# Block means of the values in two column groups of TensorE, gathered by two copies a head pair

## Chip, cores, metric

One core of a Trainium2 chip runs the whole kernel. The metric is device time in microseconds (us) of one execution; lower is better. Besides the time, every execution has a mean granted TensorE clock: 1.0 is full speed. Values of 0.997 to 0.999 in the profiled runs are a half-clock stretch at the very end (in the kernel before, from 253.70 us of 254.62 on); they count as full clock.

## The reference, cut to what matters

```python
k_sum = k.reshape(B, H, nb, block, D).max(axis=3)      # (B, H, S, D) = (4, 8, 768, 64)
v_sum = v.reshape(B, H, nb, block, D).mean(axis=3)     # block = 32, nb = 24
scores = [masked scores with 15 neighbours each way, scores with k_sum + log(block)]
attn   = softmax(scores) @ concat([v, v_sum])
...    # then x = attn as (3072, 512), and a GEGLU block with a gated residual:
out    = x + sigmoid(x @ w_res) * ((gelu(x @ w_gate) * (x @ w_val)) @ w_out)
```

The change concerns `v_sum` of the first batch only: 24 means of 32 rows for each of 8 heads.

## The kernel before

A query tile has 128 "keys": 96 real ones (64 and 16 on each side, the rims) and 32 rows of which 24 are the block means. The first batch is prepared by hand in a prologue, before the steady run of gate and value matmuls (`g`, `vv`) starts. The block means of a head pair are 12 accumulating matmuls; `bmat` is a shifted selection matrix, so that they arrive in rows 96 to 119 of a PSUM tile:

```python
def vsum_pair(hp, pool, tag):                       # L278
    vs = pool.tile([128, 512], F32, tag=tag, name="vs")
    hs = slice(2 * hp, 2 * hp + 2)
    for t in range(NT):                             # NT = 12
        nc.tensor.matmul(vs[:, 0:2 * D], bmat[:, t:t + 4, :], vext[0][0:QT, t, hs, 0:D],
                         start=(t == 0), stop=(t == NT - 1))
    nc.scalar.copy(vblk[96:128, hs, 0:D], vs[96:128, 0:2 * D].rearrange("p (h d) -> p h d", d=D))

# order of issue in the prologue (cut; each engine runs its own part in this order)
s_step(0, 0, st) ... s_step(0, 1, st, tiles=s1)     # scores (PE), exp (ACT) -> P
keep_warm(2, *t_bank)                               # 2 filler matmuls, 512 columns each
vsum_pair(0, *t_bank)
s_step(0, 2, st)
keep_warm(2, *o_bank)
pair_rims(0)                                        # copies of V's rims, on VectorE
s_step(0, 3, st, MM2)
pair_rims(1)
vsum_pair(1, *o_bank)
pair_rims(2)
av_band(0); av_blk(0)                               # ao = P @ V: 96 keys, then the 32 block rows;
keep_warm(1, *t_bank)                               #   av_blk ends in rz, xn on VectorE
vsum_pair(2, *t_bank)
nc.scalar.activation(gate1[:], bias_t[0:1, :], AF.Gelu)   # loads the Gelu table early
av_band(1); av_blk(1)
...
pair_rims(3)
keep_warm(1)
av_band(2); av_blk(2)
vsum_pair(3, *o_bank)
xt_step(0, 0, st, **t_turn)                         # transposes of xn, copied by ScalarE
av_band(3)
xt_step(0, 1, st, **o_turn)
av_blk(3)
...                                                 # gate and value matmuls, xt_step 2 and 3
```

The softmax here doesn't subtract the row's maximum and nothing guards it: scores larger than these inputs give would overflow.

Of the kernel before, what the change touches and what calls it, by code (L numbers as in the profile page):

```python
# [9 lines left out]
BF16 = mybir.dt.bfloat16  # L10
# [5 lines left out]
def kernel(  # L16
# [11 lines left out]
    nc = tc.nc  # L28
    B, H, S, D = q.shape
# [9 lines left out]
    QT = 64  # L39
    NT = S // QT  # L40
    HT = NT // 2
# [11 lines left out]
    const = ctx.enter_context(tc.tile_pool(name="const", bufs=1))  # L53
# [7 lines left out]
    ps_o = ctx.enter_context(tc.tile_pool(name="ps_o", bufs=1, space=bass.MemoryType.PSUM))  # L61
# [6 lines left out]
    band = const.tile([128, 2, 128], BF16, name="band")  # L68
    vblk = const.tile([128, H, D + 1], BF16, name="vblk")
    bias_t = const.tile([128, 1], F32, name="bias_t")  # L70
    bmat = const.tile([QT, NT + 3, 32], BF16, name="bmat")
    bgrp = const.tile([QT, 3, 32], BF16, name="bgrp")
    warm = const.tile([128, 512], BF16, name="warm")
    gate1 = const.tile([1, 1], F32, name="gate1")
# [4 lines left out]
    vext = [const.tile([128, NT, H, VP], BF16, name=f"vext{i}") for i in range(2)]  # L79
# [59 lines left out]
    with tc.manual_schedule():  # L139
# [13 lines left out]
        def own_keys(m, n):  # L153
            for i in range(2):
                rows = m[i * BLK:(i + 1) * BLK]
                nc.vector.memset(bass.AP(tensor=m.tensor, offset=rows[:, 0, i:i + 1].offset,
                                         ap=[rows.ap[0], [34, n]]), 1.0 / BLK)
# [27 lines left out]
        nc.vector.memset(band[:], 0.0)  # L185
        vext_consts(0)
        nc.vector.memset(bmat[:], 0.0)
        own_keys(bmat[:, 3:, :], NT)
        nc.vector.tensor_copy(band[0:QT, 0, 33:128], ident[0:QT, 0:95])
        nc.vector.tensor_copy(band[QT:128, 0, 33:97], ident[QT:128, QT:128])  # L190
        for i, d in enumerate((1, 2, 4, 8, 15)):
# [86 lines left out]
        def vsum_pair(hp, pool, tag):  # L278
            vs = pool.tile([128, 512], F32, tag=tag, name="vs")
            hs = slice(2 * hp, 2 * hp + 2)  # L280
            for t in range(NT):
                nc.tensor.matmul(vs[:, 0:2 * D], bmat[:, t:t + 4, :], vext[0][0:QT, t, hs, 0:D],  # L282
                                 start=(t == 0), stop=(t == NT - 1))
            nc.scalar.copy(vblk[96:128, hs, 0:D], vs[96:128, 0:2 * D].rearrange("p (h d) -> p h d", d=D))

        def vsum_grp(b, pool, tag):
            vs = pool.tile([128, DM], F32, tag=tag, name="vs")
# [89 lines left out]
        def xt_step(u, ko, st, pool, tag, copy=nc.vector.tensor_copy):  # L377
            xp = pool.tile([128, TU], BF16, tag=tag, name="xp")
            for sub in range(NSUB):
                nc.tensor.transpose(xp[:, sub * 128:(sub + 1) * 128],  # L380
                                    st["xn"][:, ko, sub, :], ident[:])
            copy(st["xT"][:, ko, :], xp[:])
# [5 lines left out]
        def new_unit():  # L388
            return {"xn": upool.tile([128, KO, NSUB, 128], BF16, tag="xn", name="xn"),
                    "xT": upool.tile([128, KO, TU], BF16, tag="xT", name="xT")}  # L390


        def gv_mm(ps, w, st, fo, kos):
            for ko in kos:
                nc.tensor.matmul(ps[:, 0:TU], w[:, ko, fo * 128:(fo + 1) * 128], st["xT"][:, ko, :],  # L395
                                 start=(ko == 0), stop=(ko == KO - 1), skip_group_check=True)
# [75 lines left out]
        def keep_warm(n, pool=ps_s, tag="s"):  # L472
            wp = pool.tile([128, 2 if pool is ps_s else 1, 512], F32, tag=tag, name="wp")
            for _ in range(n):
                nc.tensor.matmul(wp[:, 0], warm[:, 0:128], warm[:], start=True, stop=True)

        mm, t_bank, o_bank = (ps_mm, "mm"), (ps_t, "t"), (ps_o, "ao")
        keep_warm(12)
        tk, tq, ao = {}, {}, {}
# [11 lines left out]
        st = new_unit()  # L491
        gvT = upool.tile([128, FO, TU], BF16, tag="gvT", name="gvT")

        def ao_tile(hp):
            ao[hp] = ps_mm.tile([128, NSUB, 2, D + 1], F32, tag="mm", name="ao")
# [14 lines left out]
        s_step(0, 1, st, tiles=s1)  # L510
        ao_tile(0)
        ao_tile(1)
        keep_warm(2, *t_bank)
        vsum_pair(0, *t_bank)
        s_step(0, 2, st)
        keep_warm(2, *o_bank)
        pair_rims(0)
# [4 lines that stand above are left out]
        av_band(0)  # L522
        av_blk(0)
        keep_warm(1, *t_bank)
        vsum_pair(2, *t_bank)
        nc.scalar.activation(gate1[:], bias_t[0:1, :], AF.Gelu)
        av_band(1)
# [8 lines left out]
        o_turn = dict(pool=ps_o, tag="ao", copy=nc.scalar.copy)  # L536
# [6 lines left out]
        def gv_part(fo, ko):  # L543
            gv_mm(gv[fo][0], w_gate, st, fo, (ko,))
            gv_mm(gv[fo][1], w_val, st, fo, (ko,))
# [2 lines left out]
        xt_step(0, 2, st, **t_turn)  # L548
        gv_part(0, 1)
        gv_mm(gv[1][0], w_gate, st, 1, (0, 1))  # L550
        xt_step(0, 3, st, **o_turn)
        gv_part(0, 2)
        gv_mm(gv[1][1], w_val, st, 1, (0, 1))
        gv_part(0, 3)
# [100 lines left out]
        for u in range(NU):  # L655
# [57 lines left out]
            else:  # L713
                nst = new_unit()
                (mid_out if u else first_out)(u, st, gvT, nst)
                st = nst
# [30 lines left out]
```

## Time and profile before

| | before |
|---|---|
| time | 256.33 us (256.27 to 256.56) |
| span of the profiled run, mean granted clock | 254.6 us, 0.998 |
| TensorE busy | 246.6 us (97%) |
| block means (vs) on the chain of waits | 1.2% |
| first gate matmul of the steady part | 20.98 us |

The chain of waits is read backward from the last instruction: each step names what released it. A timeline row is start, length, engine, line, operation, tiles and count; a bracket at its end is the engine's idle time before it and what ended it. The prediction shows the rows. Two more of TensorE's timeline of the kernel before are needed for the comparison below, the last band product of the prologue and the first gate matmul:

```profile
20.09 0.38 PE L367 MATMUL ao<-vext,P 96*64 96x65 bf16 x12
20.98 0.34 PE L395 MATMUL g<-xT,w_gate 128*128 128x384 bf16 x1
```

No bracket: TensorE had not stood idle.

### The profile page before, as it was taken

To read this page: it belongs to the slowest core of one execution; us is meant where nothing else is said; L and a number is where in the kernel's file an instruction comes from. 1 tells how busy PE (TensorE), PEld (TensorE's weight loads), DVE (VectorE), ACT (ScalarE), POOL (GpSimd) and SP (SyncE) were. 2 spreads that over 40 slices of the span, in tenths; PEclk is the share of its full clock that TensorE was granted. 3 is DMA by queue.
4 is the path that set the end of the run, shared out by engine and by line. 5 is a ranking of instruction groups with operands and counts; after the bars stand their busy time and mean duration, and the time that the engine had idled before them with its cause. 6 is when DMAs were issued, how large, how long until landed. Compare 5 with 4: busy or idle time off the path is not lost.

```text
span 254.6 us, 5847 instructions
## 1 busy us (share of the span) xinstructions
PE 246.6 (97%) x2303; PEld 139.7 (55%) x2328; DVE 159.4 (63%) x364; ACT 129.6 (51%) x216; POOL 97.3 (38%) x128
## 2 busy tenths in 40 slices
PE   6999999999999999999999999999999999999994
PEld 2676555565545665446544665446545555456544
DVE  6985796397667544858567544958567544854424
ACT  8885468366572337353572337254572337353320
POOL 8895542361506970274406970274404000000000
PEclk9999999999999999999999999999999999999999
DMA  5999999999404999399404999289604400230003
GB/s 80 177 182 197 197 205 207 175 176 222 61 19 121 159 150 150 56 161 171 103 18 120 162 155 153 49 162 170 104 18 115 98 3 0 50 139 0 3 1 124
DMA packets 98107, 29.34 MB, mean 115 GB/s; under 512 B 83224, under 2 KB 94944, under 8 KB 97984
## 3 DMA queue, kind: packets, MB, share of 16 engines
q0 software_dynamic: 68352, 14.76, 66.3%
q1 hardware_dynamic: 29728, 14.21, 25.7%
q8 instruction: 18, 0.29, 0.5%
q14 instruction: 9, 0.07, 0.1%
HBM read 29.36 MB, written 6.29 MB: 140 GB/s over the span
## 4 chain that ended last, share of the span: by engine, by line
PE 93%; DVE 5%; issue 2%; DVEq 0%
PE g L395 25%; PE vv L395 24%; PE f L443 23%; PE r L433 8%; PE s L317 3%; PE ao L355 3%; PE vs L282 1%; PE ao L367 1%; PE tp L220 1%; PE vs L290 1%; DVE ks L237 1%; PE xp L380 1%; DVE o L452 1%; DVE th L449 1%; PE gv L395 1%
## 5 line engine op out<-in xcount | busy, mean ns | idle before, releaser
L401 DVE TENSOR_TENSOR gvT<-ge,vv 128x384 bf16<-128x384 f32 x95 | 52.2, 552 | 48.1 <-PE vv L395 43.9
L400 ACT ACTIVATE ge<-g 128x384 f32<-128x384 f32 x95 | 46.7, 491 | 67.3 <-DVE gvT L401 34.8
L395 PE MATMUL g<-xT,w_gate 128*128 128x384 bf16 x380 | 78.0, 326 | 0.0
L395 PE MATMUL vv<-xT,w_val 128*128 128x384 bf16 x380 | 77.8, 326 | 0.0
L443 PE MATMUL f<-w_out,gvT 128*128 128x512 bf16 x262 | 62.7, 379 | 1.5 <-issue 1.1
L395 PEld LDWEIGHTS <-w_gate 128*128 128x128 bf16 x384 | 37.1, 98 | 26.2 <-issue 1.4
L395 PEld LDWEIGHTS <-w_val 128*128 128x128 bf16 x384 | 37.6, 98 | 24.7
L443 PEld LDWEIGHTS <-gvT 128*128 128x128 bf16 x276 | 25.7, 98 | 29.5
L107 POOL DMA_DIRECT2D vext<-in_v_dram x32 | 24.1, 777 | 15.0 <-DMA w_out<-in_moe_w_out_dram 5.6
L436 ACT ACTIVATE th<-r 128x512 f32<-128x512 f32 x24 | 13.5, 607 | 27.6 <-PE r L433 27.6
L449 DVE SCALAR_TENSOR_TENSOR th<-th,f 128x512 f32<-128x512 f32 (+2 forms) x26 | 16.6, 640 | 14.4 <-PE f L443 14.4
L341 DVE TENSOR_TENSOR P<-P,maskt 128x768 bf16<-128x768 bf16 x28 | 16.2, 580 | 11.0 <-ACT P L337 6.1
L433 PE MATMUL r<-w_res,xT 128*128 128x512 bf16 x88 | 22.7, 380 | 0.4
L302 POOL COPY vext<-vsum 32x1536 bf16<-32x1536 bf16 x12 | 17.2, 1464 | 13.0 <-DMA vsum<-vpart 12.9
L452 DVE SCALAR_TENSOR_TENSOR o<-th,xn 128x512 f32<-128x512 f32 (+2 forms) x26 | 18.2, 701 | 0.9
L375 DVE TENSOR_TENSOR xn<-ao,rz 128x384 bf16<-128x384 f32 x32 | 17.8, 557 | 1.1
L337 ACT ACTIVATE P<-s,bias_t 128x768 bf16<-128x768 f32 x17 | 15.3, 901 | 4.5 <-PE s L317 4.3
L127 POOL DMA_DIRECT2D q_nat<-in_q_dram x18 | 15.8, 899 | 0.9 <-issue 0.7
L334 ACT ACTIVATE P<-s,bias_t 128x384 bf16<-128x384 f32 x30 | 15.7, 579 | 0.0
L237 DVE TENSOR_REDUCE ks<-kW 128x24 bf16<-128x768 bf16 x16 | 15.1, 943 | 0.0
L433 PEld LDWEIGHTS <-xT 128*128 128x128 bf16 x96 | 8.8, 98 | 9.9
L373 DVE RECIPROCAL rz<-ao 128x6 f32<-128x6 f32 x32 | 6.1, 191 | 10.9 <-PE ao L355 10.0
(90 smaller groups left out, 187.1 us busy)
## 6 DMA issues: line engine op xcount, KB each, us to landing
out_dram<-o SPq DMA_DIRECT2D x23, 256.0 KB, 2.2
vext<-in_v_dram POOLq DMA_DIRECT2D x32, 96.0 KB, 6.4
q_nat<-in_q_dram POOLq DMA_DIRECT2D x18, 128.0 KB, 6.4
w_gate<-in_moe_w_gate_dram POOLq DMA_DIRECT2D x6, 256.0 KB, 8.9
w_val<-in_moe_w_val_dram POOLq DMA_DIRECT2D x6, 256.0 KB, 9.3
w_out<-in_moe_w_out_dram POOLq DMA_DIRECT2D x3, 512.0 KB, 14.4
k_nat<-in_k_dram POOLq DMA_DIRECT2D x16, 96.0 KB, 5.8
vext<-vext SPq DMA_DIRECT2D x6, 144.0 KB, 5.4
```

Of the source, the lines that this page charges most:

```text
L107: nc.gpsimd.dma_start(out=vext[b % 2][0:QT, :, h, 0:D], in_=v[b, h].rearrange("(t p) d -> p t d", p=QT))
L237: nc.vector.tensor_reduce(out=ks.rearrange("d (t n) -> d t n", n=2), in_=kw[:, :, 0:QT].rearrange("d t (n w) -> d t n w", w=BLK), axis=myb ...
L302: eng.tensor_copy(vext[b % 2][96:128, lo:hi, :, 0:D], src)
L341: nc.vector.tensor_mul(Pf, Pf, maskt.unsqueeze(1).to_broadcast([128, 2 * HT, QT]))
L375: nc.vector.tensor_mul(xn, ao[:, :, :, 0:D], rz.to_broadcast([128, NSUB, 2, D]))
L395: nc.tensor.matmul(ps[:, 0:TU], w[:, ko, fo * 128:(fo + 1) * 128], st["xT"][:, ko, :], start=(ko == 0), stop=(ko == KO - 1), skip_group_ch ...
L400: nc.scalar.activation(ge[:], g[:, 0:TU], AF.Gelu)
L401: nc.vector.tensor_mul(gvT[:, fo, :], ge[:], vv[:, 0:TU])
L433: nc.tensor.matmul(r[:], st["xT"][:, ko, ss], w_res[:, ko, :], start=(ko == 0), stop=(ko == KO - 1))
L443: nc.tensor.matmul(st["f", sub][:], gvT[:, fo, ss], w_out[:, fo, :], start=(fo == 0), stop=(fo == FO - 1), skip_group_check=True)
L449: nc.vector.scalar_tensor_tensor(th[:, cs], th[:, cs], 1.0, f[:, 0:n], ALU.add, ALU.mult)
L452: nc.vector.scalar_tensor_tensor(o.rearrange("p (k d) -> p k d", d=128), th[:, cs].rearrange("p (k d) -> p k d", d=128), 0.5, x, ALU.mult, ...
```

## The change

It means to halve the time of the block means: weights of 32 columns instead of 128, the first six tiles in one column group of the array and the last six in another, at the same time. The two halves then lie in different rows of PSUM, so each pair is gathered by two copies on ScalarE. One filler goes, and one transpose copy moves to VectorE.

```diff
-    bmat = const.tile([QT, NT + 3, 32], BF16, name="bmat")
+    bmat = const.tile([QT, NT, 32], BF16, name="bmat")
...
-            for t in range(NT):
-                nc.tensor.matmul(vs[:, 0:2 * D], bmat[:, t:t + 4, :], vext[0][0:QT, t, hs, 0:D],
-                                 start=(t == 0), stop=(t == NT - 1))
-            nc.scalar.copy(vblk[96:128, hs, 0:D], vs[96:128, 0:2 * D].rearrange("p (h d) -> p h d", d=D))
+            for t in range(HT):
+                for g in range(2):
+                    nc.tensor.matmul(vs[96 - 32 * g:128 - 32 * g, 0:2 * D], bmat[:, g * HT + t, :],
+                                     vext[0][0:QT, g * HT + t, hs, 0:D], start=(t == 0), stop=(t == HT - 1),
+                                     tile_position=(0, 96 - 32 * g), skip_group_check=True)
+            for lo, hi in ((64, 96), (96, 96 + 2 * HT)):
+                nc.scalar.copy(vblk[96:96 + hi - lo, hs, 0:D],
+                               vs[lo:hi, 0:2 * D].rearrange("p (h d) -> p h d", d=D))
...
-        keep_warm(2, *t_bank)
+        keep_warm(1, *t_bank)
         vsum_pair(0, *t_bank)
...
-        xt_step(0, 3, st, **o_turn)
+        xt_step(0, 3, st, ps_o, "ao")
```

More of the change, by code (lines that the diff above doesn't have):

```diff
@@ L187 @@
         nc.vector.memset(bmat[:], 0.0)
-        own_keys(bmat[:, 3:, :], NT)
+        own_keys(bmat, NT)
         nc.vector.tensor_copy(band[0:QT, 0, 33:128], ident[0:QT, 0:95])
```

## The prediction

Its sum: 1.34 + 0.22 - 0.18 = 1.38 us less work on TensorE, of which 0.6 us was to be left at the end, and 255.8 us in all. The terms rest on the trace of the kernel before: 56 ns a matmul is 0.67 us for 12 (its chain at 15.07 us), 0.26 us a copy is ScalarE's row at 14.10. That two narrow matmuls run at once is taken from the products `ao`, where those of a pair start 2 to 5 ns apart. "Drain" is a longer step from one kind of matmul to the next, 0.15 instead of 0.056 us; 0.09 us is an estimate from these two, and what TensorE does in that time no trace shows.

> **What bounds the kernel now.** I read the page's chain first, then that chain in order of time between 6 and 26 us, then each engine's timeline there.
>
> ```profile
> PE 93%; DVE 5%; issue 2%; DVEq 0%
> ```
>
> TensorE carries 93% of the chain of waits that ended last, and from 25.5 us on the chain is nothing but matmul groups end to end. So the time is "when does the steady part start, plus a fixed rest", and a gain in the prologue is kept if nothing later was waiting for something else. The change is entirely in that prologue (unit 0, batch 0). Its part of the chain, start and length in us:
>
> ```profile
> 12.33 0.55 PE wp L475 x2
> 12.93 0.72 PE vs L282 x10
> ...
> 15.07 0.67 PE vs L282 x12
> 15.74 0.95 PE ao L367 x24
> 16.69 0.04 issue
> 16.73 0.83 PE vs L282 x12
> ```
>
> The block means (vs, L282) are four groups of 12 matmuls, one per head pair. With the last group (0.77 us at 19.11) and a straggler of 0.06, they hold 3.05 us of the chain, 1.2% of the span; that is all the change can attack. "wp" are filler matmuls. The same stretch of ScalarE's timeline (start, length, what; the bracket is idle time before it):
>
> ```profile
> 12.99 1.08 ACT L334 ACTIVATE P<-s,bias_t 128x384 bf16<-128x384 f32 x2
> 14.10 0.26 ACT L284 CAST vblk<-vs 32x128 bf16<-32x128 f32 x1
> 14.38 0.90 ACT L337 ACTIVATE P<-s,bias_t 128x768 bf16<-128x768 f32 x1
> 15.18 1.05 ACT L334 ACTIVATE P<-s,bias_t 128x384 bf16<-128x384 f32 x2
> 16.25 0.26 ACT L284 CAST vblk<-vs 32x128 bf16<-32x128 f32 x1
> 17.59 0.26 ACT L284 CAST vblk<-vs 32x128 bf16<-32x128 f32 x1 [1.08 <-PE vs L282]
> 17.87 1.28 ACT L526 ACT_TABLE_LOAD   x1
> 19.17 0.20 ACT L526 ACTIVATE gate<-bias_t 1x1 f32<-1x1 f32 x1
> 19.92 0.26 ACT L284 CAST vblk<-vs 32x128 bf16<-32x128 f32 x1 [0.55 <-PE vs L282]
> 20.20 1.05 ACT L382 COPY xT<-xp 128x384 bf16<-128x384 bf16 x2
> ```
>
> ScalarE has no gap from 12.99 to 16.51: the exponentials fill it. Only after that does it twice wait for the block means (1.08 and 0.55 us). So TensorE has little slack against ScalarE: it can arrive earlier for the third and fourth gather, but hardly for the first two. VectorE is as full until 17.7 us, with the rims of V that the attention matmuls (ao) need:
>
> ```profile
> 14.30 0.43 DVE L269 COPY vext<-vext 16x768 bf16<-16x768 bf16 x1
> ...
> 19.42 0.49 DVE L269 COPY vext<-vext 16x768 bf16<-16x768 bf16 x1
> ```
>
> These are the last rim copies of pair 0 (done 14.73; ao for pair 0 starts at 15.67) and of pair 3 (done 19.91; its ao starts at 20.09, almost directly).
>
> [...] The attention matmuls are already in two column groups of 64: 12 of 65 columns start within 0.31 us (below), 26 ns each, so in pairs. And from the last vs matmul of a group to the first ao it is 0.15 us instead of 0.056, so a drain is about 0.09 us. [...] the trace's cast of 32 rows took 0.26, so I charge 0.26 for the copy of 12 rows too.
>
> ```profile
> 15.67 0.38 PE L367 MATMUL ao<-vext,P 96*64 96x65 bf16 x12
> 15.98 0.37 PE L367 MATMUL ao<-vblk,P 32*64 32x65 bf16 x12
> ```
>
> **The change part by part.**
> - *Matmuls in pairs.* Count and moving width stay at 48 and 128 columns; weights shrink from 128 to 32 columns, and two run at once. 12 x 56 = 0.67 us become 6 x 56 = 0.34 us: 0.33 a pair of heads, 1.34 in all.
> - *Mode switches.* Scores (128 weight columns) and block means had one mode and followed each other without a break. Now means 0 to scores 2 and scores 3 to means 1 each get a drain: 2 x 0.09 = 0.18 us lost. The others were there already.
> - *One filler fewer.* 512 columns, 0.22 us, directly ahead of means 0, which wait for the filler to finish. Their V heads had landed by 12.04, so this moves all that follows.
> - Sum on TensorE: 1.34 + 0.22 - 0.18 = 1.38 us less work.
> - *Gathers.* Four copies become eight. The two of one pair write the same rows of vblk, so the second follows the first. Dependent pairs on VectorE (rz, then xn) have 0.03 between end and start, so one gather goes from 0.26 to about 0.55, that is +0.29; with a semaphore wait on itself (0.17 before a memset of VectorE's, L143) it would be +0.4.
> - *The fourth transpose copy* (xT, 0.48 on ScalarE) goes to VectorE, where the one such copy later took 0.36. It ended at 22.98 and the next matmul, g, began at 23.03, some 0.08 late: that wait goes.
> - bmat's memset shrinks by a fifth of 0.26 us: 0.05 of VectorE early on, which I don't count.
>
> Now which wait ends last. Means 0 start at 12.71, end at 13.05; scores 2 at 13.14; two fillers; scores 3 at 14.15 (their keys are ready at 13.89); means 1 at 14.59 to 14.93; ao of pair 0 at 15.02 (rims at 14.73, gather 0 at 14.65). That is 0.65 earlier than 15.67. Then means 2 at 16.08 and the first half of ao 1 at 16.51. Its second half needs gather 1. ScalarE: P1 ends at 14.07, gather 0 until 14.65, P2 and P3 until 16.52, gather 1 until 17.09. So this half starts at 17.17 instead of 16.82: 0.35 us of the gain is handed to the gather. Before it began at 17.80, so 0.63 is left. From there ao 2 is at 17.80, means 3 at 18.42, the first transposes at 18.85. The rims of pair 3 come from a VectorE that itself waits for ao 1; they end at 19.28, so ao 3 begins at 19.37 rather than 19.12. ScalarE does gather 2 until 17.66, the table load and gate until 19.18, gather 3 until 19.75. The second transposes (they write the bank that gather 3 empties) start at 19.84, against 20.40 before; the first gate matmul at about 20.42, against 20.98. Gain there 0.56; with the 0.08 of the moved copy 0.6 us. Of 1.38 us taken off TensorE, some 0.8 turn into waits for ScalarE and VectorE. 256.33 - 0.6 = 255.7; as the gathers may cost +0.4 rather than +0.29, I put 255.8.
>
> **The rivals.**
> *TensorE's whole 1.4 to 1.5 us arrive at the end* (254.9). For it: TensorE's share of the chain. Against it: no idle ScalarE before 16.51.
> *The gathers eat everything* (256.3 or a little above): eight copies with semaphore waits add up to 4 x 0.4 = 1.6 us of ScalarE, against a table load that cannot start before gather 2 is done. Against it: ScalarE's waits of 1.08 and 0.55 us give the slack for most of that.
> *The weights' DMAs become the bound.* If TensorE is earlier, the weights must have landed. The last w_val load is issued at 23.24 and its kind takes at most 11.2 us, so 34.45; its first use is at about 36.1. 1.65 us of margin is more than the whole gain. I give this little.
> *The granted clock falls* because the array is half empty more often: it is 1.00 in all windows from 6 us on, and TensorE is never idle for over 0.4 us. Unlikely, but it would cost more than a microsecond.
>
> **Range and chances.** The best case takes off 1.4 us, 0.5% of the time; the worst plausible adds a few tenths. The runs before spread by 0.3 us. I take 255.2 to 256.5. A change of 2% would be 5.1 us, more than the whole of the block means: same 0.985.
>
> **What would show it right or wrong.** Right: groups of vs in about 0.34 us; eight casts of 0.26; a wait of TensorE (ao for pair 1, at about 17) on the gather, where now it has none; the table load no earlier than 17.6; the first g at 20.3 to 20.7; the rest of the chain as before, moved by one constant. Wrong if the pairs don't overlap (a group still 0.67), if the two copies lie much further apart than 0.03 us, or if the gain at the first g is lost again by 40 us to a weight load.

## The result, and the profile after

The changed kernel took 257.73 us (257.56 to 258.18, four runs) against 256.34 us (four runs). The ratio is 1.0055, with a 95% interval of 1.0038 to 1.0073: half a per cent slower. A ratio here is the mean time of one kernel's fast runs over that of the other's of the same rounds, so it is not quite the ratio of the medians quoted. Within 2% it counts as the same, but the sign is clear of the noise of that session, and it is not the predicted one.

TensorE's timeline of the changed kernel, the rows that answer to those above:

```profile
14.61 0.51 PE L283 MATMUL vs<-vext,bmat 64*32 64x128 bf16 x12
15.46 0.38 PE L371 MATMUL ao<-vext,P 96*64 96x65 bf16 x12 [0.35 <-DVE vext L269]
...
18.95 0.34 PE L384 MATMUL xp<-ident,xn 128*128 128x128 bf16 x3
19.99 0.38 PE L371 MATMUL ao<-vext,P 96*64 96x65 bf16 x12 [0.70 <-DVE vext L269]
...
21.13 0.50 PE L399 MATMUL g<-xT,w_gate 128*128 128x384 bf16 x1
21.43 0.53 PE L399 MATMUL vv<-xT,w_val 128*128 128x384 bf16 x1
```

Three things are to be seen. The block means do run in pairs: a group shows 0.51 us where it showed 0.83 (both include the tail of the last matmul, whose record is 0.22 us long though the next starts 0.056 after it). Now TensorE waits for VectorE's rim copies, 0.35 us ahead of the first band product and 0.70 ahead of the last, so the last starts at 19.99 instead of 20.09: the freed time is nearly gone. These are the last rim copies of pair 0 and of pair 3 in this run; in the kernel before they took 0.43 and 0.49 us and ended at 14.73 and 19.91:

```profile
14.69 0.71 DVE L269 COPY vext<-vext 16x768 bf16<-16x768 bf16 x1
...
19.34 0.60 DVE L269 COPY vext<-vext 16x768 bf16<-16x768 bf16 x1
```

And then single gate matmuls show 0.50 to 0.53 us instead of 0.33 and start 0.32 apart instead of 0.16. That is not a wait. The sums by stretch say what it is. First the row of the kernel before, then that of the changed kernel; columns are the stretch, its length, busy time (and count) of TensorE, its weight loads, VectorE, ScalarE and GpSimd, then the granted clock, the DMA share and GB/s:

```profile
20.40:23.90 3.50, 3.50 (x42) 2.30 (x38) 1.08 (x3) 2.21 (x5) 2.21 (x3) 1.00 1.46 196
```

```profile
18.00:20.40 2.40, 1.70 (x53) 1.40 (x54) 2.23 (x7) 2.19 (x5) 1.49 (x3) 1.00 1.44 201
20.40:23.90 3.50, 3.50 (x28) 2.14 (x28) 1.11 (x3) 0.96 (x2) 2.10 (x3) 0.51 1.46 194
```

TensorE is called fully busy in both, yet does 28 matmuls instead of 42, because its granted clock was halved (0.51 in the mean of that stretch, against 1.00). The trace's record of the clock has it at half from 20.42 us on for 3.41 us. Half speed for 3.41 us costs 1.71 us of TensorE's work (an estimate, 0.5 x 3.41). The stretch before it (18.00 to 20.40) is one in which TensorE worked 1.70 of 2.40 us. All four runs of the changed kernel had a mean clock of 0.987 or 0.993; one such spell of half clock is 0.5 x 3.41 / 256 = 0.0067 of the mean, so 0.993 is one spell and 0.987 two, by this estimate.

From there on the two kernels run alike: the first matmul of the fourth part of the first gate group starts at 24.41 us against 23.03, that is 1.38 later, and the whole is 257.73 - 256.34 = 1.39 later.

### The profile page after: what moved, and what is told of

The parts are those of the page before. It is cut to its first block, busy times and chain, and to the rows that moved or that the text cites. A ratio compares the mean times of both kernels' runs of the same rounds, so it can differ in the third digit from the quotient of the medians.

```text
span 256.0 us, 5874 instructions
## 1 busy us (share of the span) xinstructions
PE 250.2 (98%) x2327; PEld 139.5 (55%) x2327; DVE 159.9 (62%) x365; ACT 130.0 (51%) x219; POOL 96.5 (38%) x128
## 4 chain that ended last, share of the span: by engine, by line
PE 92%; DVE 5%; issue 1%; ACT 0%; DVEq 0%
PE g L399 25%; PE vv L399 24%; PE f L447 24%; PE r L437 8%; PE ao L359 3%; PE s L321 3%; PE wp L479 2%; DVE ks L237 1%; PE tp L220 1%; PE vs L294 1%; DVE vext L272 1%; PE xp L384 1%; DVE o L456 1%; DVE th L453 1%; PE gv L399 1%
## 5 line engine op out<-in xcount | busy, mean ns | idle before, releaser
L399 PE MATMUL g<-xT,w_gate 128*128 128x384 bf16 x380 | 78.8, 328 | 0.0
L447 PE MATMUL f<-w_out,gvT 128*128 128x512 bf16 x276 | 64.6, 380 | 0.0
## 6 DMA issues: line engine op xcount, KB each, us to landing
out_dram<-o SPq DMA_DIRECT2D x23, 256.0 KB, 2.2
w_gate<-in_moe_w_gate_dram POOLq DMA_DIRECT2D x6, 256.0 KB, 9.0
w_val<-in_moe_w_val_dram POOLq DMA_DIRECT2D x6, 256.0 KB, 9.5
```

The costliest lines, as they stand in the source:

```text
L399: nc.tensor.matmul(ps[:, 0:TU], w[:, ko, fo * 128:(fo + 1) * 128], st["xT"][:, ko, :], start=(ko == 0), stop=(ko == KO - 1), skip_group_ch ...
L447: nc.tensor.matmul(st["f", sub][:], gvT[:, fo, ss], w_out[:, fo, :], start=(fo == 0), stop=(fo == FO - 1), skip_group_check=True)
```

## The experiments

What is to be told apart: A, the clock falls because TensorE has too little to do in a stretch. B, because of the column groups as such (fewer columns at work). C, because of the filler that was dropped. D, on what the freed time waits at full clock: VectorE's rims or ScalarE's gathers. "Clock" below is the mean granted clock of each execution; 0.993 or less means at least one half-clock spell of 3.41 us. The kernel before ran beside each session: 40 executions with a listed clock, of which four were at 0.987 (259.3 to 259.8 us) and the others mostly at 256.2 to 256.9 (seven at 257.0 to 258.0, though at 0.997 to 1.0). So the loss of clock is an event that the kernel before can have too; its frequency is what has to be compared, and beside it the times at full clock.

**Fillers in the last gap.**

```diff
+        keep_warm(3)
         av_band(3)
```

> The changed kernel with three filler matmuls in the 0.9 us in which TensorE stood idle ahead of the last band product (ao, pair 3). Theory A (the half clock from 20.5 to 23.9 us was set off by TensorE's idleness before it): the clock stays at 1.00 there, and 1.5 to 1.7 us come back: 256.0 to 256.3 us. Theory B (the column groups themselves lower the activity that keeps the clock up): the clock still drops, 257.4 to 258 us. If the clock plays no part at all: 257.7 us with the clock at 1.00.

Two runs at clock 1.00 took 255.97 and 255.99 us, two at 0.986 took 258.92 and 259.08. At full clock this beats the kernel before. As a cure it is not clear: half of four runs lost clock, and where, no trace of those two shows.

**The kernel before with an idle gap at the same place** (a block-max reduction whose result is not used, 0.94 us, on VectorE ahead of the last rims).

```diff
+        nc.vector.tensor_reduce(out=dly..., in_=kW[0][:, :, 0, 0:QT]..., op=ALU.max)
         pair_rims(3)
```

> The kernel before (no column groups) with one extra VectorE reduction of 0.93 us ahead of the rims of pair 3, so that TensorE stands idle for about 0.9 us at the same place. Theory A: the clock halves after the gap here too, and the time is 256.3 + 0.9 + 1.6 = about 258.8 us. Theory B: no drop, 257.2 us. If VectorE isn't what the band product waits for: 256.3 us.

256.94, 257.21 and 257.53 us at 0.998 to 1.0, and 258.72 at 0.993. The band product waited for the rims as meant, so VectorE does hold it. But the gap alone brought the clock down in only one of four. One gap (0.56 us idle in the profile), in an otherwise full stretch, does not regularly do it.

**The dropped filler put back.**

```diff
-        keep_warm(1, *t_bank)
+        keep_warm(2, *t_bank)
         vsum_pair(0, *t_bank)
```

> The changed kernel with the one filler matmul that it dropped put back. Theory A: the gap ahead of the last band product is set by VectorE and stays at 0.9 us; the clock still drops: 257.5 to 257.9 us. Theory C (the dropped filler is what let the clock fall): clock at 1.00, 256.1 to 256.4 us.

One run at 0.993 (257.83 us), three at 0.998 to 0.999 (255.63, 256.06 and 256.31). The profiled run was the slow one, with the half clock from 20.39 us for 3.41 us, just as in the changed kernel. So the clock can fall with the filler in place. That one of four is less than four of four says little, as the session was another. C falls as a sole cause by later runs: three variants without this filler, but with full-width block means, kept their clock in 18 of 18 executions (table below).

**The rims of pair 3 earlier on VectorE**, ahead of the normalisation of pair 1.

```diff
+        pair_rims(3)
         av_band(1)
         av_blk(1)
...
-        pair_rims(3)
```

> The changed kernel with the rims of pair 3 moved on VectorE's queue ahead of the normalisation of pair 1, so that they end at about 19.1 instead of 19.9 us. Theory A and D (VectorE's queue, not the gathers on ScalarE, holds back TensorE's freed time): the gap shrinks to 0.2 us, the clock stays up, and TensorE is 0.4 to 0.8 us earlier than before at the first gate matmul: 255.4 to 255.9 us. If the gathers hold it: 256.2 us with the clock up.

255.84, 255.97 and 255.98 us at full clock, one run at 0.987 (258.56). TensorE's timeline of the profiled run, second transposes and first gate matmul:

```profile
19.84 0.33 PE L384 MATMUL xp<-ident,xn 128*128 128x128 bf16 x3 [0.21 <-ACT vblk L287]
...
20.40 0.34 PE L399 MATMUL g<-xT,w_gate 128*128 128x384 bf16 x1
```

With the rims out of the way, the wait that ends last there is that of the transposes on the second copy of gather 3, and the first gate matmul is 0.58 us earlier than before. Against the changed kernel at full clock (20.50, in the next run) it is only 0.10 earlier. So of D's two it is VectorE's queue that ends last in the changed kernel, with ScalarE's gathers close behind.

**The changed kernel again, unedited.**

> The changed kernel once more, unedited, six executions. So far every kernel has executions with a mean granted clock of 0.998 to 1.0 and others with 0.993 or 0.987; here we learn how often. If the loss of clock is brought on by the change: at least 3 of 6 at 0.993 or below, at 257.4 us or more; the others at 255.7 to 256.3 us. If the first four (all at 0.987 to 0.993) were chance: as rare as in the kernel before (1 of 11 so far).

255.85 us at clock 1.0; the other five at 0.993 (257.54, 257.73) and 0.987 (258.38 to 258.93). With the first four, 9 of 10 executions lost clock. This time the profiled run is the one at full clock, and it shows what the change does by itself:

```profile
19.60 0.38 PE L371 MATMUL ao<-vext,P 96*64 96x65 bf16 x12 [0.28 <-DVE vext L269]
...
20.50 0.34 PE L399 MATMUL g<-xT,w_gate 128*128 128x384 bf16 x1
```

The first gate matmul is 0.48 us earlier than before, and the run 0.5 us faster (a single execution).

**The kernel before, with its full-width block means, without six fillers.**

```diff
-        keep_warm(2, *t_bank)
         vsum_pair(0, *t_bank)
...
-        keep_warm(2, *o_bank)
...
-        keep_warm(1, *t_bank)
         vsum_pair(2, *t_bank)
...
-        keep_warm(1)
         av_band(2)
```

> The kernel before, full-width block means, without its six filler matmuls (1.3 us of TensorE, about what the change takes away) between 12 and 19 us. If the clock falls because TensorE has too little to do in a stretch (theory A): 0.993 or below in at least 3 of 6, at 257.4 us or more, though no column group is there. If the column groups lower the clock (theory B): clock as in the kernel before, 255.9 to 256.4 us.

All six runs lost clock: 0.980 to 0.987, 258.17 to 259.84 us. The profiled run had half clock from 17.35 us for 6.83 us, two such spells in a row:

```profile
15.00:18.00 3.00, 2.42 (x63) 1.89 (x64) 2.35 (x6) 2.39 (x6) 2.13 (x4) 0.89 1.55 193
18.00:20.40 2.40, 2.40 (x40) 2.07 (x39) 2.23 (x7) 1.03 (x3) 2.09 (x3) 0.50 1.47 204
20.40:23.90 3.50, 3.50 (x38) 2.21 (x38) 1.08 (x3) 1.69 (x4) 1.92 (x3) 0.50 1.45 193
```

The block means have no column groups in this kernel (the products `ao` have two of 64 columns, as in every kernel here); it only has less work for TensorE: 6 x 0.216 = 1.30 us (in the trace of the kernel before, fillers in a row start 0.216 us apart), about the 1.38 us that the change removes. Column groups are not needed for the loss of clock (B falls as a necessary cause), and too little work is enough.

**The changed kernel with eight more fillers**, spread over the same stretch (1.7 us).

```diff
-        keep_warm(1, *t_bank)          # ahead of means 0
+        keep_warm(3, *t_bank)
-        keep_warm(2, *o_bank)
+        keep_warm(3, *o_bank)
-        keep_warm(1, *t_bank)          # ahead of means 2
+        keep_warm(2, *t_bank)
-        keep_warm(1)                   # ahead of the band product of pair 2
+        keep_warm(2)
+        keep_warm(3)                   # ahead of that of pair 3
```

> The changed kernel with its column groups and eight more filler matmuls (1.7 us) spread over the same stretch, so that TensorE is as busy as before. Theory A: no or one execution of 6 below 0.998, and 256.0 to 256.5 us. Theory B: clock as in the changed kernel, at least 3 of 6 at 0.993 or below.

Six of six at clock 1.0, 256.59 to 256.99 us. From 15 to 18 us TensorE was busy for 2.79 us, against 2.42 in the last run (which had its clock halved for the end of that stretch):

```profile
15.00:18.00 3.00, 2.79 (x87) 2.08 (x86) 2.38 (x6) 2.53 (x7) 2.20 (x4) 1.00 1.54 194
```

The column groups are all there, and the clock stays up: this and the last run, of one session, are the pair that decides for A against B. Each filler is a matmul on the whole array (128 rows, 128 columns), so the pair doesn't tell whether it is the time with work that counts or the share of the array at work. All six took longer than the 256.0 to 256.5 us that I expected, and than the kernel before in the median (256.74 against 256.5): eight fillers are too many, and the first gate matmul came at 21.52 us.

**The changed kernel with full-width block means**, all else kept (two copies included).

```diff
-            for t in range(HT):
-                for g in range(2): ... tile_position=(0, 96 - 32 * g)
-            for lo, hi in ((64, 96), (96, 96 + 2 * HT)): ...
+            for t in range(NT): ...                 # as before
+            for n in (32, 2 * HT):                  # the second copy repeats 12 rows
+                nc.scalar.copy(vblk[96:96 + n, hs, 0:D], vs[96:96 + n, 0:2 * D]...)
```

> The changed kernel with the block means at full width again, everything else kept (one filler fewer, two copies a pair, the fourth transpose copied by VectorE). Theory A: the gap ahead of the last band product is a few tenths at most, clock at 0.998 or more in at least 5 of 6, 256.0 to 256.5 us. If the double copies, and not the column groups, cost the time: 256.6 us or more at full clock.

No loss of clock in six: 256.12 to 256.27 us four times, 256.74 and 256.96. So the doubled copies cost nothing that shows (the filler that is left out, 0.22 us, could hide a little), and of the change's parts it is the halved matmuls that let the clock fall; that they do so through the work that they leave out is taken from the pair above.

**The best version: rims first, and three fillers where TensorE waits anyway.**

```diff
         pair_rims(2)
+        keep_warm(1, *t_bank)
         av_band(0)
...
+        pair_rims(3)
         av_band(1)
...
-        pair_rims(3)
...
+        keep_warm(1)
         vsum_pair(3, *o_bank)
...
         av_band(3)
+        keep_warm(1)
         xt_step(0, 1, st, **o_turn)
```

> The changed kernel with the rims of pair 3 first (as in the earlier run, 255.84 to 255.98 us at full clock, but one of four executions at 0.987) and three fillers put where TensorE waits anyway: ahead of the band product of pair 0, ahead of the block means of pair 3, and after the band product of pair 3. If a stretch too empty is what lowers the clock and these places have room: clock at 0.998 or more in at least 5 of 6, 255.8 to 256.1 us. If the places have no room: 256.2 to 256.5 us at full clock. If three fillers are too few: 2 or more of 6 below 0.998.

No loss of clock in six, median 255.98 us (255.74 to 256.42) against 256.59 (256.28 to 257.39) beside it; ratio 0.9974, interval 0.9957 to 0.9991. It beats the kernel before by about a quarter of a per cent (by the interval, 0.1 to 0.4), and beats by more the nine executions of the changed kernel that lost clock. The first gate matmul, in its profile:

```profile
20.52 0.34 PE L399 MATMUL g<-xT,w_gate 128*128 128x384 bf16 x1
```

That is as early as in the changed kernel at full clock, and 0.12 us later than with the rims first and no fillers (20.40): three fillers, 0.65 us of work, cost 0.12.

**Rims first, and only one of the two copies** (wrong result: 12 of the 24 means stay zero).

```diff
-            for lo, hi in ((64, 96), (96, 96 + 2 * HT)):
+            for lo, hi in ((64, 96),):
```

> The changed kernel with the rims of pair 3 first and only the first of the two gather copies of each pair (wrong result on purpose: the first 12 block means of each head stay zero). With the rims out of the way, the second transposes waited for the second copy of gather 3. If the gathers are the next bound, as the prediction had it: executions at full clock are 0.2 to 0.5 us faster than the 255.84 to 255.98 us with both copies, 255.4 to 255.7 us, and the wait of the transposes on the gather goes. If they are not: 255.8 to 256.0 us.

Four of six lost clock (258.50 to 258.61 us); two at 1.0 took 255.92 and 256.17. At full clock there is no gain over two copies (255.84 to 255.98 us, in an earlier session). The wait on the gather is gone from the profile, but that profile fell in a run at half clock from 17.56 us on, so what took its place at full clock I can't show.

**The fourth transpose copied by ScalarE again**, in the full-width variant.

```diff
-        xt_step(0, 3, st, ps_o, "ao")
+        xt_step(0, 3, st, **o_turn)
```

> The full-width variant of the changed kernel (256.1 to 256.3 us mostly) with the fourth transpose copied by ScalarE again. If moving that copy is worth the 0.08 us that the prediction gave it: 256.2 to 256.4 us, and a short wait of TensorE ahead of the last part of the first gate group. If nothing: the same as with VectorE.

256.17 to 256.59 us, median 256.34, against 256.23 (another session). That would fit 0.1 us, but it lies within the spread of each: not settled.

**The scheduling of the best version without column groups**: the kernel before with rims first, one filler fewer, and the fourth copy on VectorE.

> The kernel before (full-width block means, one copy a pair) with the scheduling alone of the best version: rims of pair 3 first, one filler fewer, the fourth transpose copied by VectorE. If the column groups are what gives the best version its gain (TensorE itself sets the end of the stretch here): first gate matmul at 20.7 to 20.8 us, 256.0 to 256.3 us, clock at 0.998 or more in at least 5 of 6. If the order of the rims alone does it: 255.7 to 256.0 us.

256.22 to 257.0 us, median 256.47, against 256.63 beside it; ratio 0.9983, interval 0.9940 to 1.0026, no loss of clock in six; first gate matmul at 20.75. So without the column groups no gain is to be told from noise, while with them the first gate matmul is at 20.52.

All together, TensorE's work in the prologue against the kernel before (a filler is 0.216 us), and the executions with a clock of 0.993 or less:

| kernels | work, us | lost clock |
|---|---|---|
| kernel before | 0 | 4 of 40 |
| full width, one filler fewer (three variants) | -0.22 | 0 of 18 |
| column groups and eight fillers | +0.35 | 0 of 6 |
| gap alone | 0 | 1 of 4 |
| column groups and three fillers (two variants) | -0.73 | 2 of 10 |
| changed kernel; filler back; rims first; one copy | -1.16 to -1.38 | 9 of 10; 1 of 4; 1 of 4; 4 of 6 |
| before without six fillers | -1.30 | 6 of 6 |

With 1.1 us or more taken out, 21 of 30 lost clock; otherwise 7 of 78. These sums mix sessions on different chips, so look within each too. In the second session of experiments the changed kernel and the one without six fillers lost clock in 11 of 12, the other three in 2 of 23. In the third, the one-copy kernel did in 4 of 6, the others in 0 of 23. In the first, filler back and rims first lost it in 2 of 8, fillers in the last gap in 2 of 4, the gap alone and the kernel before in 2 of 11: by itself that session decides nothing.

## Why the prediction was wrong

Step by step, as the prediction put them:

- *Block means in pairs, 0.34 us a group.* Right: matmuls of a pair start 2 to 18 ns apart, pairs about 56 ns, and groups shrank by 0.32 us. The two longer steps that it put at 0.09 us each are there too: from means 0 to scores 2 it is 0.148 us, from scores 3 to means 1 0.120, where the steps within these groups are about 0.056 and 0.026.
- *Gathers of about 0.55 us, table load no earlier than 17.6.* Right. ScalarE's timeline of the changed kernel:

```profile
16.57 1.12 ACT L287 CAST vblk<-vs 32x128 bf16<-32x128 f32 x4
17.71 1.28 ACT L530 ACT_TABLE_LOAD   x1
```

- *The second half of ao 1 waits 0.35 us for gather 1.* Wrong. VectorE's rims had stopped TensorE earlier: the first band product, put at 15.02, started at 15.46, so gather 1 was ready. The term that was mis-sized is the rim copies. I took their lengths from the one profile of before (0.35 and 0.43 us for the first two); in the changed kernel they took 0.69 and 0.71. That profile already had one of 0.71, at 14.77. In the fourteen traces 26 of 112 rim copies of the first batch took 0.59 to 0.72 us. All 26 ran beside one of GpSimd's instructions that issue the weights' DMAs (L164) for 70% of their time or more, but so did most of the short ones; the cause was not tested.
- *Rims of pair 3 end at 19.28, ao 3 begins at 19.37, first gate matmul at about 20.42.* Nearly right at full clock: ao 3 at 19.60, gate at 20.50. So was the sum: one clean run of 255.85 us against a predicted 255.8. That it fits so well is luck in part: the forecast wait of 0.35 us on gather 1 was not there, and one of 0.25 on the rims of pair 0 (at 15.29) stood in its place. The last wait is on VectorE's rims, 0.28 us; with the rims first, one of 0.21 on ScalarE's gather took its place.
- *"The granted clock falls because the array is half empty more often [...] Unlikely, but it would cost more than a microsecond."* **This is the step that failed.** It was named and set aside, with the argument that TensorE is never idle for over 0.4 us. That was true of the kernel before, not of the changed one: the same text predicted that 0.8 us of TensorE's freed time would turn into waits, and did not ask what these waits would do to the clock. The cause that it named is not shown either: the kernel without six fillers lost its clock with full-width block means, and the one with eight fillers kept it with column groups. What the runs show is that too little work brings the clock down (6 of 6 executions of the kernel before without six fillers lost it, none of 6 of the changed kernel with eight more); whether as time or as share of the array stays open. "More than a microsecond" was an estimate with no trace behind it. Of the changed kernel, 9 of 10 executions had mean clocks that fit one or two half-clock spells of 3.41 us each, at up to 1.71 us; 255.85 + 1.71 = 257.56, where the runs at 0.993 took 257.54 to 257.74.
- *DMAs of the weights.* Rightly dismissed; the shift of 1.38 us at the gate matmuls was still there at the end.

The fillers are called "keep_warm"; what they do for the clock is known here from the runs alone. It takes no long idle gap to lose it: the longest wait of TensorE between 12 us and the fall was 0.70 us in the profiled run of the changed kernel and 0.52 us in that of the kernel without six fillers, and the clock fell in both. A stretch that is merely thin is enough.

When it falls was only observed. In the fourteen profiled runs the first full clock came between 3.9 and 7.1 us after the start, differently from run to run (4.53 in the kernel before, 6.77 in the changed one). In the four traces with a loss, the clock fell 13.65 us after that (changed kernel, filler back, one copy) or 10.24 us (without six fillers), four and three times 3.41. At the same two distances from its own first full clock, the run of the changed kernel that kept its clock comes to 15.98 and 19.39 us (an estimate, worked out from its trace), the one that lost it to 17.01 and 20.42. That such a difference decides which execution of ten keeps its clock is the author's guess; no run shows it. How much work it takes to keep the clock stays open too: from 15 to 18 us TensorE was busy for 2.36 us in the run that kept it and for 2.60 in the one that lost it at 20.42, and I found no count of busy time that separates the 3.41 us before every fall from all others.

## What to carry to other kernels

Before taking work off a busy engine, ask what it waits for next: here 1.38 us less on TensorE was worth 0.5 us at full clock. If that engine is TensorE, ask also whether the stretch becomes thin enough to lose its clock (here 21 of 30 executions did with 1.1 us or more of work taken out, and 7 of 78 otherwise), and look at the granted clock of every execution, not only at one profile: a gain of 0.5 us and a loss of 1.7 us were both the same kernel. Filler matmuls put mostly into waits that exist anyway made the change a gain, of a quarter of a per cent.
